# Two-step logits, a reordered stage-out, a split first chunk and a last block in pieces, in a TensorE-bound attention + MLP kernel

## The chip, the cores and the metric

One core of a Trainium2 chip. The metric is the device time of one execution in microseconds (us), as the median of several runs. The profile's span is about 1.7 us shorter than the time of the same run; I compare times with times and spans with spans.

## The reference, cut to what matters

```python
xn = layernorm(x)                              # x: 1 x 2048 x 1024
out = x + A(xn) + B(xn)
# A: 32 heads of 32, four segments of 512 tokens; per segment and head
#    p = softmax(q k^T * scale + causal mask); a_dot = p v
#    a_mem = phi(q) M / (phi(q) z);  M, z summed over earlier segments
#    o = g * a_mem + (1 - g) * a_dot;  A = o @ wo
# B: token-mixing MLP: u = gelu(layernorm(xn)^T w1 + b1); B = (u w2 + b2)^T
```

## The kernel before

TensorE (PE) computes the hidden layer first. Then come 32 units, each of four heads in one segment. Between the short pieces of a unit's attention the kernel places the long matmuls of w2 and wo ("main" matmuls), so that PE has work while ScalarE does exps. `share(u)` says how many main matmuls go into each gap. Main block c (128 tokens) sums half 0 in bank 6 and half 1 in bank 7; VectorE then drains each into a staging tile.

The logits of a unit use row tiles: head r occupies rows 32r to 32r+31 of the array, so four matmuls of 32 rows run at once (in the timeline below, four start within 0.01 us of each other). Key block kb has 128 keys and 512 - 128 kb queries. Before the change a unit has three such steps, all in banks 0 to 3, one bank a head. In the code, cut and shortened, `weigh` is the product of p and v:

```python
LOGIT_STEPS = [[0], [1], [2, 3]]
def logits(self, u, step):
    ...
    with fw.group(reads=[kT[k], qT[k]], writes=self.R_bank[0:4]):
        for kb in kbs:
            for r in range(4):
                fw.mm(self.ps[:, r, col:col + n_q], kT[32r:32r+32, kb*P:(kb+1)*P],
                      qT[32r:32r+32, kb*P:SEG_L], ..., tile_position=(32 * r, 0))
    # one exp of ScalarE per step, then one causal select of POOL per key block
# ... one unit:
self.logits(u, 0);  self.main_emit(n0)
self.logits(u, 1);  self.main_emit(n1)
self.logits(u, 2);  self.main_emit(n2)
self.weigh(u, 0); self.weigh(u, 1)     # banks 4 and 5
self.proj_q(un, 0)                     # bank 0
self.weigh(u, 2); self.proj_v(..., 2); self.weigh(u, 3)
self.proj_k(un, 1)                     # bank 1; VectorE copies k, then ScalarE takes exp(k)
self.main_emit(n3)                     # then the next unit's logits
```

The end of the kernel is eight products of o and wo in blocks of 128 tokens by 512 columns; VectorE adds each to what was staged out, and a DMA writes it. The start loads x in chunks; VectorE computes the statistics and writes h, and ten matmuls on zeros (the warm-ups) run on PE meanwhile.

The softmax here doesn't subtract the row's maximum and nothing guards it: scores larger than these inputs give would overflow.

Of the kernel before, what the change touches and what calls it, by code (L numbers as in the profile page):

```python
# [6 lines left out]
ACT = mybir.ActivationFunctionType  # L7
ALU = mybir.AluOpType
# [8 lines left out]
SEG_L = 512  # L17
# [12 lines left out]
N_UNIT = N_SEG * N_GRP  # L30
VW = D_HEAD + 1
GW = 4 * VW
PT_OFF = [0, 512, 896, 1152]
PT_COLS = 1280


# [66 lines left out]

class FW:
    N_DMA_SEMS = 64
    N_OUT_SEMS = 24
    N_OWN_SEMS = 16

    def __init__(self, nc, ctx):
# [236 lines left out]
class _Kernel:  # L346
# [31 lines left out]
    def alloc(self):  # L378
# [49 lines left out]
        self.w1early = nc.alloc_sbuf_tensor_at("w1early", [P, N_TCH, 512], BF16, offset=w1_at)  # L428
        self.late_end = e.at
        self.R_xin = [Res(f"xin{c}") for c in range(N_TCH)]  # L430
        self.R_xin0 = Res("xin0a")
        self.R_junk, self.R_warm = Res("junk"), Res("warm")
        self.R_h = [[Res(f"h{c}_{h}") for h in range(2)] for c in range(N_TCH)]
        self.R_hh = [[self.R_h[c][h] for c in range(N_TCH)] for h in range(2)]
# [79 lines left out]
    def consts(self):  # L514
        fw = self.fw
        fw.op("dve", lambda e: e.memset(self.warm[:], 0.0), writes=[self.R_warm])
        for brow, R in ((self.brow1, self.R_brow1), (self.brow2, self.R_brow2)):
            fw.op("dve", lambda e: e.memset(brow[:], 0.0), writes=[R[4]])
        self.w1_ring = _Ring(fw, [t[:] for t in self.w1ring], self.R_w1s, depth=2)
        for fp in range(N_FCH // 2):  # L520
            self.w1_ring.srcs.append(self.B_w1[:, fp * 256:(fp + 1) * 256].rearrange("(c p) f -> p c f", p=P))
        self.R_w1e = [Res(f"w1e{c}") for c in range(N_TCH)]
        for h in range(2):
            fw.dma(self.xin[:, 0, h * 512:(h + 1) * 512], self.x_d[:, 0, h * 512:(h + 1) * 512],
                   writes=[(self.R_xin0, self.R_xin[0])[h]], issuer=("sp", "act")[h])
        fw.op("act", lambda e: e.activation(self.junk[:, 0:1], self.warm[:, 0:1], ACT.Gelu_apprx_tanh),
              reads=[self.R_warm], writes=[self.R_junk])
        for kind, c0, n in (("x", 1, 1), ("x", 2, 1), ("x", 3, 1), ("w", 0, 2), ("x", 4, 2), ("w", 2, 2), ("x", 6, 2),
                            ("w", 4, 4), ("x", 8, 4), ("w", 8, 4), ("x", 12, 4), ("w", 12, 4)):
            if kind == "x":  # L530
                self.load_x(c0, n)
            else:
                self.fw.dma(self.w1early[:, c0:c0 + n, :],
                            self.B_w1[c0 * P:(c0 + n) * P, 0:512].rearrange("(c p) f -> p c f", p=P),
                            writes=self.R_w1e[c0:c0 + n], issuer="act" if c0 == 0 else "sp")
        self.w1_ring.issued = 2
        for brow, src, n, R in ((self.brow1, self.B_b1, N_FCH, self.R_brow1), (self.brow2, self.B_b2, N_TCH, self.R_brow2)):
            for j in range(4):
                fw.dma(brow[32 * j:32 * j + n, :], src.rearrange("(c q) -> c q", q=P)[:, 32 * j:32 * j + 32],
                       reads=[R[4]], writes=[R[j]])  # L540
        fw.dma(self.beta_sb[:], self.A_beta.partition_broadcast(P), writes=[self.R_beta])

        fw.op("pool", lambda e: e.memset(self.expo[:], -0.5), writes=[self.R_expo])
        fw.op("pool", lambda e: e.memset(self.ident[:], 0.0), writes=[self.R_ident])
        fw.op("pool", lambda e: e.affine_select(self.ident[:], self.ident[:], pattern=[[-1, P]],
                                                compare_op=ALU.not_equal, fill=1.0, base=0,
                                                channel_multiplier=1),
              reads=[self.R_ident], writes=[self.R_ident])
        with fw.group(reads=[self.R_warm], writes=[self.R_bank[0]]):
            for _ in range(self.N_WARM):  # L550
                fw.mm(self.bank(0), self.warm[:, 0:P], self.warm[:], start=True, stop=True)
# [65 lines left out]
    def stats_dve(self, c, halves):  # L617
        fw = self.fw
        src, st, R = self.xin[:, c, :], self.ln_st[:, c, :], self.R_st[c]
        for h in halves:  # L620
            R_x = self.R_xin0 if c == 0 and h == 0 else self.R_xin[c]
            fw.op("dve", lambda e: e.bn_stats(st[:, 6 * h:6 * h + 6], src[:, 512 * h:512 * h + 512]), reads=[R_x],
                  writes=[R])
        if halves[-1]:
            fw.op("dve", lambda e: e.bn_aggr(self.ln_mv[:, c, :], st.rearrange("p (a s) -> p a s", s=6)),
                  reads=[R], writes=[R])
# [29 lines left out]

    def scale_h(self, c):
        reads = [self.R_xin[c], self.R_st[c], self.R_rs[c]]
        for h0, h1 in ((0, 1), (1, 2)) if c == 1 else ((0, 2),):
            cols = slice(512 * h0, 512 * h1)  # L660
            self.fw.op("dve", lambda e: e.tensor_scalar(self.h[:, c, cols], self.xin[:, c, cols], self.ln_mv[:, c, 0:1],  # L661
                                                        self.ln_rs[:, c, 1:2], op0=ALU.subtract, op1=ALU.mult),
                       reads=reads, writes=self.R_h[c][h0:h1])
# [111 lines left out]
        self.fw.dma(self.pk[j][:], self.mtmp[1][:], reads=[self.R_mtmp[1]], writes=[self.R_pk[j]], transpose=True)  # L775


    LOGIT_STEPS = [[0], [1], [2, 3]]

    def logits(self, u, step):  # L780
        fw = self.fw
        k = u % 3
        kbs = self.LOGIT_STEPS[step]
        total = sum(SEG_L - P * kb for kb in kbs)
        with fw.group(reads=[self.R_kT[k], self.R_qT[k]], writes=self.R_bank[0:4]):
            col = 0
            for kb in kbs:
                n_q = SEG_L - P * kb
                for r in range(4):
                    fw.mm(self.ps[:, r, col:col + n_q], self.kT[k][32 * r:32 * r + 32, kb * P:(kb + 1) * P],  # L790
                          self.qT[k][32 * r:32 * r + 32, kb * P:SEG_L],
                          start=True, stop=True, tile_position=(32 * r, 0))
                col += n_q
        off = PT_OFF[kbs[0]]
        fw.op("act", lambda e: e.activation(self.pT[:, :, off:off + total], self.ps[:, 0:4, 0:total],  # L795
                                            ACT.Exp, scale=SCALE),
              reads=self.R_bank[0:4],
              writes=[self.R_pTu[kb] for kb in kbs] + [self.R_pTd[kb] for kb in kbs])
        for kb in kbs:
            d = self.pT[:, :, PT_OFF[kb]:PT_OFF[kb] + P]  # L800
            fw.op("pool", lambda e: e.affine_select(d, d, pattern=[[0, 4], [1, P]], compare_op=ALU.is_ge,  # L801
# [95 lines left out]
    def main_init(self):  # L897


        self.main = []  # L900
        for j, c in enumerate(self.mlp_order):
            self.main += [(j, c, half, a, a + 14) for half in range(2) for a in (0, 14)]
            if c < 12:
                self.main += [(j, c, half, N_FCH, N_FCH + N_GRP) for half in range(2)]
        self.main_k = 0
        self.main_at = 0

# [38 lines left out]
    def attention_and_out(self):  # L946
# [17 lines left out]
        for u in range(N_UNIT):  # L964
            s = u // N_GRP
            un, m = u + self.LEAD, u // 4 + 1
            n0, n1, n2, n3 = self.share(u)
            if u == N_GRP:
                wait = _after(*[self.R_xnT[c] for c in range(4)])
                self.oT[1] = self.xnT[0]  # L970
# [5 lines left out]
            if u and not last_of_seg(u - 1):  # L976
                self.combine(u - 1)
            self.logits(u, 1)
            self.main_emit(n1)
            self.logits(u, 2)  # L980
            if u + 1 < N_UNIT and (u + 1) // N_GRP < N_SEG - 1:
                self.k_transpose(u + 1)
            if u and not last_of_seg(u - 1):
                self.o_transpose_dma(u - 1)
            self.main_emit(n2)
            self.weigh(u, 0)
            self.weigh(u, 1)
            if un < N_UNIT:
# [8 lines left out]
                self.proj_k(un, 1)  # L997
            if last_of_seg(u):
                self.combine(u)
            self.main_emit(n3)  # L1000
        assert self.main_k == len(self.main)
        self.tail()

    @staticmethod
    def share(u):

        if u < N_UNIT - 4:
            return (10, 8, 7, 7) if u < N_GRP else (10, 8, 8, 8)
        return (10, 9, 8, 10) if u < N_UNIT - 2 else (10, 9, 8, 4)

    def tail(self):
        fw = self.fw
# [6 lines left out]
            fw.dma(fin[i][:], self.out_d[:, 4 * s + i, :], reads=[self.R_out[4 * s + i]], writes=R_fin[i],  # L1019
                   record_reads=False)  # L1020

        def product(n, j0, j1):
            i, h, b = n // 2, n % 2, (0, 1, 2, 3, 4, 5, 7, 6)[n]
            with fw.group(reads=[self.R_wo] + self.R_oT[s % 2][j0:j1], writes=[self.R_bank[b]]):
                for jc in range(j0, j1):
                    fw.mm(self.bank(b), self.oT[s % 2][:, jc, i * P:(i + 1) * P],
                          self.wo_sb[:, jc, h * 512:(h + 1) * 512], start=(jc == 0), stop=(jc == N_GRP - 1))
            if j1 < N_GRP:
                return
            dst = fin[i][:, h * 512:(h + 1) * 512]  # L1030
            fw.op("dve", lambda e: e.tensor_tensor(dst, self.bank(b), dst, op=ALU.add),  # L1031
                  reads=[self.R_bank[b], R_fin[i][h]], writes=[R_fin[i][h]])
            fw.dma(self.out_d[:, 4 * s + i, h * 512:(h + 1) * 512], dst, reads=[R_fin[i][h]],
                   writes=[self.R_out[4 * s + i]], is_output=True)

        product(0, 0, 7)
        product(1, 0, 7)
# [1 line left out]
        product(2, 0, 7)  # L1039
        for n in range(3):  # L1040
            product(n, 7, 8)
        for n in range(3, 8):
            product(n, 0, 8)


# [26 lines left out]
```

## Time and profile before

| | before |
|---|---|
| time, median of the first 3 runs | 704.21 us (703.87 to 705.7) |
| span of the profile | 702.2 us |
| PE busy | 688.9 us (98%) |
| first real matmul | 7.14 us |
| last PE work to end of span | about 3 us |

PE is the only engine near its limit. From the page (part 1, and the chain of work that ended last; PE is TensorE's matmuls, PEld its weight loads, DVE VectorE, ACT ScalarE, POOL GpSimd, SPq and ACTq the queues that issue DMAs, x the number of instructions):

```profile
PE 688.9 (98%) x4724; PEld 322.7 (46%) x4814; DVE 258.5 (37%) x578; ACT 277.5 (40%) x301; POOL 100.8 (14%) x156
...
PE 95%; DMA 1%; issue 1%; DVE 1%; SPq 0%; ACT 0%; ACTq 0%
```

"Busy" hides short gaps and waits, because matmul records overlap: a dense full matmul of 512 columns is recorded with 0.38 us, but the next one starts 0.216 us later. Start times do not hide them. Here are the three logits steps of a unit in segment 2, by the timeline (start, us busy, engine, line, operation, tiles, count, and the idle time before with what ended it):

```profile
486.04 0.10 PEld L194 LDWEIGHTS ps_all<-qT_1549,kT_1552 32*128 32x128 bf16 x4 [0.42 <-issue]
486.04 0.40 PE L194 MATMUL ps_all<-qT_1549,kT_1552 32*128 32x512 bf16 x4
486.37 1.90 PE L194 MATMUL ps_all<-gT,w2h_896 128*128 128x512 bf16 x8
...
488.64 0.34 PE L194 MATMUL ps_all<-qT_1549,kT_1552 32*128 32x384 bf16 x4
488.91 1.90 PE L194 MATMUL ps_all<-gT,w2h_895 128*128 128x512 bf16 x8
...
490.74 0.34 PE L194 MATMUL ps_all<-qT_1549,kT_1552 32*128 32x256 bf16 x8
```

The four tiled matmuls of a step start within 0.01 us of each other. The last full matmul before the step started 0.312 us earlier (single records; 0.216 when dense). The tiles' 512 columns need 0.213 us (a step with 128 columns fewer is 0.053 us shorter), yet the next full matmul starts 0.33 us after their start. So each step costs about 0.21 us beside its columns, 0.096 us on entry (0.312 less 0.216) and about 0.115 us on exit; the texts call an entry with its exit a switch.

One wait of PE on another engine stands out. It is in the chain between 377 and 381 us (start, us, what):

```profile
377.27 0.70 DVE kT_1552 L755
...
378.06 0.61 ACT etmp_1566 L758
...
378.69 0.30 DVE mtmp_1568 L726
...
379.62 0.75 DVE stg_1573 L939
...
380.51 0.59 PE ps_all L194 x2
...
PE ps_all L194 <- DVE stg_1573 L939: 0.7, 1, 0.7
```

Half 0's drain (`stg`) sits in VectorE's queue behind the copy of k and work that waits for ScalarE's exp. PE needs bank 6 for the next block and waits (0.85 us by start times; the last line is from the waits view: us in total, times, longest).

The end, by the timeline: the last add starts at 699.27 us; its transfer is issued and lands, and the span ends at 702.2.

```profile
696.70 2.54 PE L194 MATMUL ps_all<-wo_sb,xnT_70 128*128 128x512 bf16 x11
...
699.27 0.69 DVE L1031 TENSOR_TENSOR fin_7784<-ps_all,fin_7784 128x512 bf16<-128x512 f32 x1 [1.03 <-PE ps_all L194]
```

### The profile page before, as it was taken

The page shows a single profiled execution, that of the slowest core. Times are in us where ns is not written, and L with a number is a line of the kernel's source. Part 1 is how long each engine was busy: PE and PEld are TensorE (multiplying, and loading weights), DVE is VectorE, ACT ScalarE, POOL GpSimd, SP SyncE. Part 2 cuts the span into 40 slices and gives each one's busy share as a digit, 9 for nine tenths or more (in the row PEclk, how much of TensorE's full clock was granted, in tenths as well). Part 3 has the DMA queues.
Part 4 walks back from the last instruction along what each step waited for, and adds up shares of the span by engine and source line. Part 5 has one row for each costly group of instructions (what it writes and reads, how often), then busy time and mean ns, then how long its engine had stood idle before and what let it go on. Part 6 is the DMA issues. An engine that isn't in the chain of part 4 may idle for free.

```text
span 702.2 us, 11155 instructions
## 1 busy us (share of the span) xinstructions
PE 688.9 (98%) x4724; PEld 322.7 (46%) x4814; DVE 258.5 (37%) x578; ACT 277.5 (40%) x301; POOL 100.8 (14%) x156
## 2 busy tenths in 40 slices
PE   8999999999999999999999999999999999999998
PEld 3444444444444444444444444444444444444443
DVE  7730000000012333343454454545546553434444
ACT  7522111111134445444544444444444444443440
POOL 3600000000001111211121211112211111211120
DMA  9497694226044537556264543526173444537003
GB/s 323 98 225 176 139 234 125 61 60 139 1 159 92 114 60 145 120 94 118 50 133 98 112 100 75 128 46 143 34 170 88 86 95 78 114 69 120 23 16 135
DMA packets 210393, 77.17 MB, mean 110 GB/s; under 512 B 172840, under 2 KB 202792, under 8 KB 210344
## 3 DMA queue, kind: packets, MB, share of 16 engines
q1 hardware_dynamic: 209928, 76.06, 47.8%
q8 instruction: 38, 0.62, 0.4%
q10 hardware_dynamic: 416, 0.39, 0.2%
q14 instruction: 11, 0.09, 0.0%
HBM read 59.79 MB, written 5.24 MB: 93 GB/s over the span
## 4 chain that ended last, share of the span: by engine, by line
PE 95%; DMA 1%; issue 1%; DVE 1%; SPq 0%; ACT 0%; ACTq 0%
PE ps_all L194 95%; DMA xin<-in_A_x_dram 1%; SPq L216 0%; DVE prod L873 0%; DVE stg_1573 L939 0%; DVE stg_1571 L939 0%; DVE kT_1552 L755 0%; DVE fin_7784 L1031 0%; DVE ost_1562 L835 0%; ACT etmp_1566 L758 0%; DVE h L661 0%; DVE o_s_1564 L877 0%; PE ps_all L200 0%; DVE srec L871 0%; DVE mtmp_1568 L726 0%
## 5 line engine op out<-in xcount | busy, mean ns | idle before, releaser
L795 ACT ACTIVATE pT<-ps_all 128x1536 bf16<-128x1536 f32 (+1 forms) x96 | 152.9, 1593 | 93.9 <-PE ps_all L194 93.9
L801 POOL TENSOR_SCALAR_AFFINE_SELECT pT<-pT 128x512 bf16<-128x512 bf16 x128 | 84.6, 673 | 564.6 <-ACT pT L795 564.6
L717 ACT ACTIVATE gT<-ps_all,b1c 128x512 bf16<-128x512 f32 x56 | 37.7, 690 | 139.1 <-PE ps_all L194 133.6
L755 DVE CAST kT_1552<-ps_all 128x512 bf16<-128x512 f32 x11 | 7.6, 691 | 170.4 <-PE ps_all L194 170.4
L194 PE MATMUL ps_all<-h,w1s_80 128*128 128x512 bf16 x251 | 55.6, 379 | 0.3
L194 PE MATMUL ps_all<-h,w1s_81 128*128 128x512 bf16 x251 | 55.6, 379 | 0.3
L194 PE MATMUL ps_all<-h,w1s_79 128*128 128x512 bf16 x250 | 55.4, 379 | 0.3
L194 PE MATMUL ps_all<-gT,w2h_895 128*128 128x512 bf16 x219 | 55.1, 380 | 0.4 <-issue 0.2
L194 PE MATMUL ps_all<-gT,w2h_893 128*128 128x512 bf16 x220 | 53.9, 380 | 1.0 <-DVE stg_1573 L939 0.7
L194 PE MATMUL ps_all<-gT,w2h_894 128*128 128x512 bf16 x215 | 53.8, 380 | 0.9 <-issue 0.6
L194 PE MATMUL ps_all<-gT,w2h_896 128*128 128x512 bf16 x217 | 53.9, 380 | 0.6 <-issue 0.3
L835 DVE CAST ost_1561<-ps_all 128x264 bf16<-128x264 f32 (+1 forms) x64 | 23.8, 394 | 64.4 <-PE ps_all L194 64.2
L194 PEld LDWEIGHTS ps_all<-h,w1s_80 128*128 128x128 bf16 x256 | 25.0, 98 | 30.2
L194 PEld LDWEIGHTS ps_all<-h,w1s_79 128*128 128x128 bf16 x256 | 25.0, 98 | 30.2
L194 PEld LDWEIGHTS ps_all<-h,w1s_81 128*128 128x128 bf16 x256 | 25.0, 98 | 30.2
L758 ACT ACTIVATE etmp_1566<-ps_all 128x512 bf16<-128x512 f32 x24 | 14.3, 597 | 58.8 <-DVE kT_1554 L755 20.7
L835 DVE CAST ost_1562<-ps_all 128x264 bf16<-128x264 f32 (+1 forms) x64 | 23.7, 394 | 37.2 <-PE ps_all L194 37.0
L194 PEld LDWEIGHTS ps_all<-gT,w2h_893 128*128 128x128 bf16 x224 | 20.4, 98 | 26.6 <-issue 4.6
L194 PEld LDWEIGHTS ps_all<-gT,w2h_896 128*128 128x128 bf16 x224 | 20.4, 98 | 25.3 <-issue 3.5
L194 PEld LDWEIGHTS ps_all<-gT,w2h_894 128*128 128x128 bf16 x224 | 20.1, 98 | 25.2 <-issue 4.0
L194 PEld LDWEIGHTS ps_all<-gT,w2h_895 128*128 128x128 bf16 x224 | 20.0, 98 | 25.2 <-issue 4.5
L194 PE MATMUL ps_all<-wo_sb,oT_1569 128*128 128x512 bf16 x124 | 30.4, 380 | 0.3 <-issue 0.2
(154 smaller groups left out, 838.6 us busy)
## 6 DMA issues: line engine op xcount, KB each, us to landing
w1s_81<-in_B_w_dram SPq DMA_DIRECT2D x4, 1024.0 KB, 5.7
w1s_79<-in_B_w_dram SPq DMA_DIRECT2D x4, 1024.0 KB, 5.8
w1s_80<-in_B_w_dram SPq DMA_DIRECT2D x4, 1024.0 KB, 5.7
wq_889<-in_A_wq_dram SPq DMA_DIRECT2D x16, 256.0 KB, 4.5
wq_890<-in_A_wq_dram SPq DMA_DIRECT2D x16, 256.0 KB, 3.5
wk_891<-in_A_wk_dram SPq DMA_DIRECT2D x16, 256.0 KB, 4.8
wk_892<-in_A_wk_dram SPq DMA_DIRECT2D x16, 256.0 KB, 3.8
w2h_893<-in_B_w_dram SPq DMA_DIRECT2D x8, 448.0 KB, 4.8
```

The costliest lines, as they stand in the source:

```text
L194: ins = self.nc.tensor.matmul(*args, **kwargs)
L717: fw.op("act", lambda e: e.activation(self.gT[:, fc, half * 512:(half + 1) * 512], self.bank(b), ACT.Gelu_apprx_tanh, bias=self.b1c[:, fc: ...
L755: fw.op("dve", lambda e: e.tensor_copy(self.kT[k][:], self.bank(b)), reads=[self.R_bank[b]], writes=[self.R_kT[k]])
L758: fw.op("act", lambda e: e.activation(self.etmp[1][:], self.bank(b), ACT.Exp), reads=[self.R_bank[b]], writes=[self.R_etmp[1]])
L795: fw.op("act", lambda e: e.activation(self.pT[:, :, off:off + total], self.ps[:, 0:4, 0:total], ACT.Exp, scale=SCALE), reads=self.R_bank[0:4],
L801: fw.op("pool", lambda e: e.affine_select(d, d, pattern=[[0, 4], [1, P]], compare_op=ALU.is_ge, fill=0.0, base=0, channel_multiplier=-1), ...
L835: fw.op("dve", lambda e: e.tensor_copy(dst, self.ps[:, b, 0:n * VW]), reads=[self.R_bank[b]], writes=[self.R_ost[o][qb]])
```

## The change

It has four parts. (1) Two logits steps instead of three: key blocks 0 and 2, then 1 and 3. Key block 2's results go to banks 4 and 5, two heads in each. (2) Half 0's wo sum goes between the two parts of half 1's w2 sum, so bank 6 is drained earlier. (3) The first x chunk is split by partitions instead of columns over two queues, w1's first part moves to the other queue, and h of chunk 0 is written in halves. (4) The last 512 columns are computed, added and written in pieces of 256, 128 and 128.

```diff
-    LOGIT_STEPS = [[0], [1], [2, 3]]
+    LOGIT_STEPS = [[[(0, 2), (2, 2)], [(1, 0), (3, 0), (0, 0), (2, 0)], [(1, 2), (3, 2)]],
+                   [[(0, 1), (1, 1), (2, 1), (3, 1), (0, 3), (1, 3), (2, 3), (3, 3)]]]   # (head, key block)
...
+            if len(toks) == 2:        # the second pair waits for the first: same banks, other row tiles
+                fw.E["pe"].eng.wait_ge(toks[0].sem, toks[0].val)
...
-            return (10, 8, 7, 7) if u < N_GRP else (10, 8, 8, 8)
+            return (11, 14, 7) if u < N_GRP else (11, 15, 8)
...
-                self.main += [(j, c, half, N_FCH, N_FCH + N_GRP) for half in range(2)]
+                wo = [(j, c, half, N_FCH, N_FCH + N_GRP) for half in range(2)]
+                runs = runs[:3] + [wo[0], runs[3], wo[1]] if c % 4 else runs + wo
...
-            fw.dma(self.xin[:, 0, h * 512:(h + 1) * 512], ...)
+            fw.dma(self.xin[64 * h:64 * h + 64, 0, :], ...)
...
-        for h0, h1 in ((0, 1), (1, 2)) if c == 1 else ((0, 2),):
+        for h0, h1 in ((0, 1), (1, 2)) if c < 2 else ((0, 2),):
...
-        for n in range(3, 8):
+        for n in range(3, 7):
             product(n, 0, 8)
+        product(7, 0, 8, ((0, 256), (256, 384), (384, 512)))
```

More of the change, by code (lines that the diff above doesn't have):

```diff
@@ L32 @@
 GW = 4 * VW
-PT_OFF = [0, 512, 896, 1152]
+PT_OFF = [0, 768, 512, 1152]
 PT_COLS = 1280
@@ L105 @@
     N_DMA_SEMS = 64
-    N_OUT_SEMS = 24
+    N_OUT_SEMS = 26
     N_OWN_SEMS = 16
@@ L430, in alloc @@
         self.R_xin = [Res(f"xin{c}") for c in range(N_TCH)]
-        self.R_xin0 = Res("xin0a")
+        self.R_xin0 = Res("xin0b")
         self.R_junk, self.R_warm = Res("junk"), Res("warm")
@@ L522, in consts @@
         self.R_w1e = [Res(f"w1e{c}") for c in range(N_TCH)]
-        for h in range(2):
-            fw.dma(self.xin[:, 0, h * 512:(h + 1) * 512], self.x_d[:, 0, h * 512:(h + 1) * 512],
-                   writes=[(self.R_xin0, self.R_xin[0])[h]], issuer=("sp", "act")[h])
+        for h, issuer in enumerate(("sp", "act")):
+            fw.dma(self.xin[64 * h:64 * h + 64, 0, :], self.x_d[64 * h:64 * h + 64, 0, :],
+                   writes=[(self.R_xin[0], self.R_xin0)[h]], issuer=issuer)
         fw.op("act", lambda e: e.activation(self.junk[:, 0:1], self.warm[:, 0:1], ACT.Gelu_apprx_tanh),
               reads=[self.R_warm], writes=[self.R_junk])
-        for kind, c0, n in (("x", 1, 1), ("x", 2, 1), ("x", 3, 1), ("w", 0, 2), ("x", 4, 2), ("w", 2, 2), ("x", 6, 2),
+        for kind, c0, n in (("x", 1, 1), ("x", 2, 1), ("w", 0, 2), ("x", 3, 1), ("x", 4, 2), ("w", 2, 2), ("x", 6, 2),
                             ("w", 4, 4), ("x", 8, 4), ("w", 8, 4), ("x", 12, 4), ("w", 12, 4)):
@@ L534, in consts @@
                             self.B_w1[c0 * P:(c0 + n) * P, 0:512].rearrange("(c p) f -> p c f", p=P),
-                            writes=self.R_w1e[c0:c0 + n], issuer="act" if c0 == 0 else "sp")
+                            writes=self.R_w1e[c0:c0 + n])
         self.w1_ring.issued = 2
@@ L620, in stats_dve @@
         for h in halves:
-            R_x = self.R_xin0 if c == 0 and h == 0 else self.R_xin[c]
-            fw.op("dve", lambda e: e.bn_stats(st[:, 6 * h:6 * h + 6], src[:, 512 * h:512 * h + 512]), reads=[R_x],
+            reads = [self.R_xin[c]] + ([self.R_xin0] if c == 0 else [])
+            fw.op("dve", lambda e: e.bn_stats(st[:, 6 * h:6 * h + 6], src[:, 512 * h:512 * h + 512]), reads=reads,
                   writes=[R])
@@ L782, in logits, with weights @@
         k = u % 3
-        kbs = self.LOGIT_STEPS[step]
-        total = sum(SEG_L - P * kb for kb in kbs)
-        with fw.group(reads=[self.R_kT[k], self.R_qT[k]], writes=self.R_bank[0:4]):
-            col = 0
-            for kb in kbs:
-                n_q = SEG_L - P * kb
-                for r in range(4):
-                    fw.mm(self.ps[:, r, col:col + n_q], self.kT[k][32 * r:32 * r + 32, kb * P:(kb + 1) * P],
+        toks = []
+        for group in self.LOGIT_STEPS[step]:
+            if len(toks) == 2:
+                fw.E["pe"].eng.wait_ge(toks[0].sem, toks[0].val)
+            banks = self.R_bank[4:6] if group[0][1] == 2 else self.R_bank[0:4]
+            with fw.group(reads=[self.R_kT[k], self.R_qT[k]], writes=banks) as grp:
+                for r, kb in group:
+                    n_q = SEG_L - P * kb
+                    b, col = (4 + r // 2, 256 * (r % 2)) if kb == 2 else (r, 384 if kb == 3 else 0)
+                    fw.mm(self.ps[:, b, col:col + n_q], self.kT[k][32 * r:32 * r + 32, kb * P:(kb + 1) * P],
                           self.qT[k][32 * r:32 * r + 32, kb * P:SEG_L],
                           start=True, stop=True, tile_position=(32 * r, 0))
-                col += n_q
-        off = PT_OFF[kbs[0]]
-        fw.op("act", lambda e: e.activation(self.pT[:, :, off:off + total], self.ps[:, 0:4, 0:total],
-                                            ACT.Exp, scale=SCALE),
-              reads=self.R_bank[0:4],
-              writes=[self.R_pTu[kb] for kb in kbs] + [self.R_pTd[kb] for kb in kbs])
+            toks.append(grp.tok)
+        heads = self.ps[:, 0:4, :]
+        if step == 0:
+            self.weights((0,), heads, self.R_bank[0:4])
+            self.weights((2,), self.ps[:, 4:6, :].rearrange("p b (h q) -> p (b h) q", q=256), self.R_bank[4:6])
+        else:
+            self.weights((1, 3), heads, self.R_bank[0:4])
+    def weights(self, kbs, src, R_src):
+        fw = self.fw
+        off, total = PT_OFF[kbs[0]], sum(SEG_L - P * kb for kb in kbs)
+        fw.op("act", lambda e: e.activation(self.pT[:, :, off:off + total], src, ACT.Exp, scale=SCALE),
+              reads=R_src, writes=[self.R_pTu[kb] for kb in kbs] + [self.R_pTd[kb] for kb in kbs])
         for kb in kbs:
@@ L901, in main_init @@
         for j, c in enumerate(self.mlp_order):
-            self.main += [(j, c, half, a, a + 14) for half in range(2) for a in (0, 14)]
+            runs = [(j, c, half, a, a + 14) for half in range(2) for a in (0, 14)]
             if c < 12:
-                self.main += [(j, c, half, N_FCH, N_FCH + N_GRP) for half in range(2)]
+                wo = [(j, c, half, N_FCH, N_FCH + N_GRP) for half in range(2)]
+                runs = runs[:3] + [wo[0], runs[3], wo[1]] if c % 4 else runs + wo
+            self.main += runs
         self.main_k = 0
@@ L966, in attention_and_out @@
             un, m = u + self.LEAD, u // 4 + 1
-            n0, n1, n2, n3 = self.share(u)
+            n0, n1, n2 = self.share(u)
             if u == N_GRP:
@@ L978, in attention_and_out @@
             self.logits(u, 1)
-            self.main_emit(n1)
-            self.logits(u, 2)
             if u + 1 < N_UNIT and (u + 1) // N_GRP < N_SEG - 1:
@@ L984, in attention_and_out @@
                 self.o_transpose_dma(u - 1)
-            self.main_emit(n2)
+            self.main_emit(n1)
             self.weigh(u, 0)
@@ L999, in attention_and_out @@
                 self.combine(u)
-            self.main_emit(n3)
+            self.main_emit(n2)
         assert self.main_k == len(self.main)
@@ L1007, in share @@
         if u < N_UNIT - 4:
-            return (10, 8, 7, 7) if u < N_GRP else (10, 8, 8, 8)
-        return (10, 9, 8, 10) if u < N_UNIT - 2 else (10, 9, 8, 4)
+            return (11, 14, 7) if u < N_GRP else (11, 15, 8)
+        return (11, 16, 10) if u < N_UNIT - 2 else (11, 16, 4) if u < N_UNIT - 1 else (11, 13, 7)
     def tail(self):
@@ L1020, in tail, with product @@
                    record_reads=False)
-        def product(n, j0, j1):
+        def product(n, j0, j1, cols=((0, 512),)):
             i, h, b = n // 2, n % 2, (0, 1, 2, 3, 4, 5, 7, 6)[n]
-            with fw.group(reads=[self.R_wo] + self.R_oT[s % 2][j0:j1], writes=[self.R_bank[b]]):
-                for jc in range(j0, j1):
-                    fw.mm(self.bank(b), self.oT[s % 2][:, jc, i * P:(i + 1) * P],
-                          self.wo_sb[:, jc, h * 512:(h + 1) * 512], start=(jc == 0), stop=(jc == N_GRP - 1))
-            if j1 < N_GRP:
-                return
-            dst = fin[i][:, h * 512:(h + 1) * 512]
-            fw.op("dve", lambda e: e.tensor_tensor(dst, self.bank(b), dst, op=ALU.add),
-                  reads=[self.R_bank[b], R_fin[i][h]], writes=[R_fin[i][h]])
-            fw.dma(self.out_d[:, 4 * s + i, h * 512:(h + 1) * 512], dst, reads=[R_fin[i][h]],
-                   writes=[self.R_out[4 * s + i]], is_output=True)
+            for p, (c0, c1) in enumerate(cols):
+                with fw.group(reads=[self.R_wo] + self.R_oT[s % 2][j0:j1], writes=[self.R_bank[b]]):
+                    for jc in range(j0, j1):
+                        fw.mm(self.ps[:, b, c0:c1], self.oT[s % 2][:, jc, i * P:(i + 1) * P],
+                              self.wo_sb[:, jc, h * 512 + c0:h * 512 + c1], start=(jc == 0), stop=(jc == N_GRP - 1))
+                if j1 < N_GRP:
+                    return
+                dst = fin[i][:, h * 512 + c0:h * 512 + c1]
+                R = Res("fin")
+                R.w = R_fin[i][h].w
+                fw.op("dve", lambda e: e.tensor_tensor(dst, self.ps[:, b, c0:c1], dst, op=ALU.add),
+                      reads=[self.R_bank[b], R], writes=[R])
+                fw.dma(self.out_d[:, 4 * s + i, h * 512 + c0:h * 512 + c1], dst, reads=[R],
+                       is_output=True, issuer=("sp", "act")[p % 2])
+                b = (b + 1) % 3
         product(0, 0, 7)
```

## The prediction

> **What bounds the kernel now.** TensorE. The page gives PE 688.9 us busy of a 702.2 us span (98%), ACT 40%, DVE 37%; the chain of work that ended last is 95% PE. By start times in the timeline, full matmuls follow each other every 0.216 us from 7.14 us on. Beside that there is little: 7.1 us ahead of the first real matmul; entries to and exits from the row-tiled logits; one PE wait of 0.7 us for a stage-out add of VectorE (waits view, at 380 us); 0.4 us before the last transposes; 2.9 us after PE's last matmul.
>
> **The logits.** A unit has three row-tiled steps. The last full matmul before a step starts 0.312 us before the first tiled one (0.216 in dense streaming); the next full matmul comes 0.105 us later than the tiles' streaming accounts for, its successor 0.01 late: 0.21 us a step, 96 steps, 20 us. [...] The change has two steps: 32 x 0.21 = 6.7 us removed. The streamed columns stay 1280 per tile.
>
> But the new first step holds a wait: key block 2's four heads share banks 4 and 5, and the second pair waits for the first's completion[...]. A tiled 256-column matmul takes 0.277 us to its end, plus 0.04 us to the waiter (as PE to ACT shows), so the second pair starts 0.32 us into the step instead of 0.215. I estimate 0.10 to 0.15 us returned per unit, 3.2 to 4.8 us. Net gain: 2 to 3.5 us.
>
> Exps: 1.88 + 1.45 + 1.45 us become 1.88 + about 1.0 + 1.88, the same sum; by my estimate ScalarE frees the banks 0.5 us before step two needs them, and POOL's selects (0.63 us each) are done 0.5 us before the weighing. No effect.
>
> **Stage-out order.** With the first half's wo sum amid the second half's w2, bank 6 is drained long before it is needed: the 0.7 us wait (0.85 in the start gap) goes.
>
> **Start.** The first chunk was already on two queues; a split by partitions should land alike (3.64 and 3.82 us before). Statistics now need both halves (up to 0.15 us later); the first half of h takes 0.36 instead of 0.53 us. w1's first part, now behind x chunk 2, should land near 5.9 us, in time. First matmul 0.0 to 0.3 us earlier, 0.1 expected; PE is dense after it.
>
> **Tail.** The last add shrinks from 0.69 us (512 columns) to about 0.22 (128), the last transfer from 128 to 32 KB saves perhaps 0.1, narrow matmuls cost 0.06: 0.5 us. The 0.4 us before the transposes stays.
>
> **Sum.** 704.2 - 2.7 - 0.8 - 0.1 - 0.5 = about 700.1 us; 697.2 to 703.2 should hold it. Within 2%: 0.97; faster by over 2%: 0.02; slower: 0.01.
>
> **Checks.** Right: two switches a unit; each first step's last pair about 0.32 us after the first; unit period 0.06 to 0.11 us shorter; no PE wait at 380 us; PE end to span end 2.4 us. Wrong: the inner wait costs over 0.2 us (no gain) or nothing (gain near 6 us); PE waiting for ACT or POOL at step two or the weighing; a later first matmul.
>
> **What would break it.** A slower restart after the inner wait; POOL selects of 0.9 us, seen sometimes, delaying the weighing; the earlier stage-out add delaying the key copy and thereby the next logits.

The sum: 2.7 + 0.8 + 0.1 + 0.5 = 4.1 us off 704.2, about 700.1. The 0.21 us was read from the trace; that the second pair has to wait was the premise, and no run tested it. The wait's 0.277 and 0.04 us can be read in the trace of before: a tiled matmul of 256 columns is recorded with 0.277 to 0.278 us, and ScalarE starts 0.04 to 0.05 us after the PE work it waits for. The terms of the tail were estimates, without their source: 0.22 us for the last add, 0.1 for the transfer, 0.06 for the narrow matmuls. The traces of before and after show 0.29 us for the add, 0.24 less from its end to the end of the span (2.24 to 2.00), and 0.04 more for the matmuls (eight times 0.109 + 2 x 0.056 us from start to start, against eight times 0.216).

## The result, and the profile after

The changed kernel took 699.52 us (median of 4 runs, 698.74 to 700.99) against 704.77 (703.87 to 705.7). The ratio is 0.9928, interval 0.9904 to 0.9951. A ratio here is the mean time of one kernel's runs over that of the other's of the same rounds, so it is not quite the ratio of the medians. The gain is 0.7%, within the 2% to which the prediction gave 0.97. The two profiled spans are 702.2 and 698.3 us.

PE's busy time, from the page, hardly moved:

```profile
PE 687.9 (99%) x4740; PEld 327.3 (47%) x4830; DVE 260.3 (37%) x581; ACT 273.9 (39%) x301; POOL 104.8 (15%) x156
```

The gain is in gaps. The waits view of PE no longer has the stage-out add (line: who waited for whom, us in total, times, longest):

```profile
PE ps_all L194 <- DVE h L661: 1.5, 1, 1.5
PE ps_all L194 <- DVE brow_51 L518: 1.3, 1, 1.3
PE ps_all L200 <- DVE o_s_1566 L890: 0.5, 1, 0.5
PE ps_all L194 <- issue: 0.3, 2, 0.2
```

The two steps of a unit in segment 2, by the timeline:

```profile
574.61 0.11 PEld L194 LDWEIGHTS ps_all<-qT_1551,kT_1554 32*128 32x128 bf16 x6 [0.42 <-DVE srec L885]
574.61 0.63 PE L194 MATMUL ps_all<-qT_1551,kT_1554 32*128 32x256 bf16 x8
574.95 0.09 PEld L194 LDWEIGHTS ps_all<-qT_1551,kT_1554 32*128 32x128 bf16 x2 [0.24 <-PE ps_all L194]
575.15 2.79 ACT L810 ACTIVATE pT<-ps_all 128x2048 bf16<-128x2048 f32 x2 [3.98 <-PE ps_all L194]
575.17 0.98 PEld L194 LDWEIGHTS ps_all<-gT,w2h_895 128*128 128x128 bf16 x6
...
577.65 0.40 PE L194 MATMUL ps_all<-qT_1551,kT_1554 32*128 32x384 bf16 x8
...
577.98 0.82 PE L194 MATMUL ps_all<-gT,w2h_896 128*128 128x512 bf16 x3
```

Step one shows the wait inside: six weight loads run at once, two come 0.34 us later, released by PE itself. That is the second pair, waiting for the first. The releaser in the first line (a small VectorE operation) is a guess of the profile; the 0.42 us there is the same at every entry.

From the single matmul records, per unit: three entries of 0.312 us and three steps of 0.327, 0.274 and 0.276 us (first tiled start to next full start) became two entries of 0.312 and two steps of 0.561 and 0.330. After a step the next full matmul takes 0.226 instead of 0.216 us. Together 3 x (0.312 - 0.216) + 0.877 + 0.030 = 1.195 us became 2 x 0.096 + 0.891 + 0.020 = 1.103: 0.092 us less a unit, 2.9 us in 32 units.

The unit period (start of a unit's logits to the next) confirms it in segments 1 and 2: 15.19 to 15.09 us. In segment 0 it fell by more, 14.65 to 14.43. The timeline of before shows why, in a unit of segment 0:

```profile
274.00 0.60 ACT L758 ACTIVATE etmp_1566<-ps_all 128x512 bf16<-128x512 f32 x1 [2.55 <-DVE kT_1554 L755]
...
274.71 0.13 PEld L194 LDWEIGHTS ps_all<-qT_1550,kT_1553 32*128 32x128 bf16 x4 [0.52 <-issue]
274.74 0.40 PE L194 MATMUL ps_all<-qT_1550,kT_1553 32*128 32x512 bf16 x4
```

Here the entry takes 0.432 us, not 0.312: the tiled loads wait until ScalarE has read bank 1 (274.00 + 0.60). In the changed kernel the first pair goes to banks 4 and 5, so it starts on time, and only the four matmuls behind it wait. The same place after:

```profile
274.67 0.60 ACT L758 ACTIVATE etmp_1568<-ps_all 128x512 bf16<-128x512 f32 x1 [2.55 <-DVE kT_1556 L755]
275.28 0.44 PEld L194 LDWEIGHTS ps_all<-qT_1552,kT_1555 32*128 32x128 bf16 x8 [0.42 <-issue]
275.29 0.63 PE L194 MATMUL ps_all<-qT_1552,kT_1555 32*128 32x256 bf16 x8
```

The entry is 0.311 us again, and the step is 0.561 us as in segment 2: the late bank hides behind the wait for the pair, which is there anyway. The late entry is in units 1 to 8 of the kernel before (unit 8 is the first of segment 1), 8 x 0.12 = 0.96 us. In unit 8 of the changed kernel 0.12 us come back: one start gap before a wo matmul (337.26 to 337.59 us) is 0.332 instead of 0.216 us, perhaps for a transpose of o that landed at 337.45; this was not tested. Net: 0.84 us.

The tail after:

```profile
693.63 2.36 PE L194 MATMUL ps_all<-wo_sb,xnT_70 128*128 128x512 bf16 x26
...
695.14 0.74 DVE L1047 TENSOR_TENSOR fin_7812<-ps_all,fin_7812 128x256 bf16<-128x256 f32 x2 [0.18 <-PE ps_all L194]
695.91 0.35 ACTq L216 DMA_DIRECT2D out_dram<-fin_7812  x1
696.03 0.29 DVE L1047 TENSOR_TENSOR fin_7812<-ps_all,fin_7812 128x128 bf16<-128x128 f32 x1 [0.16 <-PE ps_all L194]
```

The last add takes 0.29 instead of 0.69 us. From the last matmul's start to the end of the span 3.35 us became 2.54, but that start lies 0.20 us later after the transposes (three short pieces end later than seven full matmuls begin). Net: 0.6 us.

And the start went the wrong way. The first real matmul came at 7.20 us instead of 7.14, and the matmuls after it ran at half rate (about 0.43 us from start to start, against 0.216). The timeline of PE up to 10 us has 14 of them before and 7 after:

```profile
7.14 3.18 PE L194 MATMUL ps_all<-h,w1early 128*128 128x512 bf16 x14 [1.86 <-DVE h L661]
```

and after

```profile
7.20 3.01 PE L194 MATMUL ps_all<-h,w1early 128*128 128x512 bf16 x7 [1.49 <-DVE h L661]
```

```
start-to-start of the first real matmuls, us (from the trace's single records)
before: 7.14 | 0.215 0.215 0.215 0.215 0.215 0.216 ...
after:  7.20 | 0.38 0.43 0.43 0.43 0.43 0.43 0.33 0.22 ...
```

That cost 1.34 us in this run (36.16 us to the first matmul after the early hidden stage, where 7.20 us plus 128 matmuls at 0.216 would give 34.82).

So the work behind the start and the start itself must be read apart. The marker is the first matmul that uses the ring of w1 tiles, right after the early hidden stage. "Rest" is the span less this marker; the two profiles have 667.44 and 662.16 us, 5.28 less:

| profile | marker at | rest | rest against before |
|---|---|---|---|
| before | 34.76 | 667.44 | |
| after | 36.16 | 662.16 | -5.28 |
| logits_only | 36.40 | 663.40 | -4.04 |
| order_only | 34.71 | 666.59 | -0.85 |
| tail_only | 35.09 | 666.83 | -0.61 |
| start_only | 36.54 | 667.45 | 0.01 |
| eight_before_logits | 36.37 | 667.26 | -0.18 |
| no_second_pair | 34.74 | 658.61 | -8.83 |
| warm14 | 34.98 | 662.14 | -5.30 |
| warm4 | 36.93 | 662.15 | -5.29 |
| pair_in_step_two | 35.01 | 661.41 | -6.03 |
| start_by_columns | 34.68 | 662.13 | -5.31 |
| product_before_transposes | 35.98 | 661.68 | -5.76 |
| all_together | 34.98 | 660.97 | -6.47 |

Three profiles of the same code behind the start (after, warm14, warm4) agree within 0.03 us, so the rest can be read to some hundredths. The marker moves by over 2 us between runs.

### The profile page after: what moved, and what is told of

The parts are those of the page before. It is cut to its first block, busy times and chain, and to the rows that moved or that the text cites. A ratio compares the mean times of both kernels' runs of the same rounds, so it can differ in the third digit from the quotient of the medians.

```text
span 698.3 us, 11182 instructions
## 1 busy us (share of the span) xinstructions
PE 687.9 (99%) x4740; PEld 327.3 (47%) x4830; DVE 260.3 (37%) x581; ACT 273.9 (39%) x301; POOL 104.8 (15%) x156
## 4 chain that ended last, share of the span: by engine, by line
PE 96%; DMA 1%; issue 1%; DVE 1%; SPq 1%
PE ps_all L194 96%; DMA xin<-in_A_x_dram 1%; SPq L216 1%; DVE prod L886 0%; DVE stg_1573 L954 0%; DVE ost_1564 L848 0%; DVE h L661 0%; DVE o_s_1566 L890 0%; PE ps_all L200 0%; DVE srec L884 0%; DVE fin_7812 L1047 0%; DVE srec L883 0%; DVE srec L885 0%; DVE ln_mv L644 0%; DVE ln_st L622 0%
## 5 line engine op out<-in xcount | busy, mean ns | idle before, releaser
L810 ACT ACTIVATE pT<-ps_all 128x2048 bf16<-128x2048 f32 (+1 forms) x96 | 149.4, 1591 | 58.3 <-PE ps_all L194 57.2
L814 POOL TENSOR_SCALAR_AFFINE_SELECT pT<-pT 128x512 bf16<-128x512 bf16 x128 | 88.3, 703 | 554.8 <-ACT pT L810 553.7
L194 PE MATMUL ps_all<-gT,w2h_897 128*128 128x512 bf16 x219 | 54.3, 380 | 0.4
L194 PE MATMUL ps_all<-gT,w2h_895 128*128 128x512 bf16 x221 | 53.7, 380 | 0.2
L194 PE MATMUL ps_all<-gT,w2h_896 128*128 128x512 bf16 x214 | 53.0, 380 | 0.6 <-issue 0.2
L194 PE MATMUL ps_all<-gT,w2h_898 128*128 128x512 bf16 x215 | 52.7, 379 | 0.5 <-issue 0.2
L194 PEld LDWEIGHTS ps_all<-gT,w2h_898 128*128 128x128 bf16 x224 | 21.1, 98 | 25.5 <-issue 1.3
L194 PEld LDWEIGHTS ps_all<-gT,w2h_896 128*128 128x128 bf16 x224 | 20.9, 98 | 25.8 <-issue 1.7
L194 PEld LDWEIGHTS ps_all<-gT,w2h_895 128*128 128x128 bf16 x224 | 20.8, 98 | 25.2 <-issue 1.3
L194 PEld LDWEIGHTS ps_all<-gT,w2h_897 128*128 128x128 bf16 x224 | 20.7, 98 | 24.9 <-issue 1.3
```

The costliest lines, as they stand in the source:

```text
L194: ins = self.nc.tensor.matmul(*args, **kwargs)
L810: fw.op("act", lambda e: e.activation(self.pT[:, :, off:off + total], src, ACT.Exp, scale=SCALE), reads=R_src, writes=[self.R_pTu[kb] for ...
L814: fw.op("pool", lambda e: e.affine_select(d, d, pattern=[[0, 4], [1, P]], compare_op=ALU.is_ge, fill=0.0, base=0, channel_multiplier=-1), ...
```

## The experiments

Twelve kernels ran, in three groups. Each group shared runs of the kernel before, whose medians were 704.15, 704.12 and 705.71 us. The comparison with the reference does not vouch for small errors in the attention part.

### Each part alone, on the kernel before

The edits are the four parts of the diff above, one at a time.

> The kernel before with the two-step logits (and their shares of other matmuls) alone. My theory: per unit 0.09 us less in the switches (three entries and exits of 0.21 us become two, less 0.13 us of wait for the first pair inside step one), 2.9 us in 32 units; and in units 1 to 7 the 0.12 us wait for bank 1 (ScalarE's exp of the k projection) disappears behind the first pair, 0.8 us more: 3.5 to 4.0 us less than before in a like clock phase. If the bank wait is not part of it: 2.9 us. If the prediction's sum was right as it stood, 2 to 3.5 us. Unit period in segment 0: 14.64 to 14.43 us; in segment 1: 15.19 to 15.10 us.

Measured: 701.58 us (699.81 to 701.88), ratio 0.9946 (0.9927 to 0.9964). Unit period 14.43 us in segment 0 and 15.09 to 15.10 in segment 1, as expected. The rest is 4.04 us shorter: 2.9 for the switches, 0.84 net for the hidden bank wait (0.12 in each of eight units, less 0.12 that unit 8 gives back, here too), and 0.23 because the stage-out wait, still there, shrank from 0.85 to 0.62 us. Both terms of the theory are confirmed; the sum of the prediction for this part, 2 to 3.5, was too small.

> The kernel before with the first half's wo sum placed amid the second half's w2 sum, alone. My theory: only the PE wait at 380 us for the stage-out add disappears, 0.85 us less; every other gap between matmul starts stays as it is. Rival: the order does nothing by itself, and the wait went because the two-step logits shifted the units' work: then within 0.2 us of before, with the wait at 380 us still in the waits view.

Measured: 704.06 us (703.04 to 705.18), ratio 0.9989 (0.9973 to 1.0006). The rest is 0.85 us shorter, the unit period that held the wait went from 16.04 to 15.19, and the waits view has no stage-out add. The order does it by itself. On top of the two-step logits it is worth what they leave, 0.62 us.

> The kernel before with the last block in column pieces alone. From the last full matmul's start, 3.34 us to the end of the span before against 2.52 us with pieces: 0.7 to 0.8 us less, of it about 0.4 the add (0.69 to 0.29 us), 0.15 the shorter matmul, 0.2 the smaller transfer. If only the add counts: 0.4 us. If the narrower pieces of 256 and 128 columns slow PE by weight loads, the gain is under 0.3 us.

Measured: 703.53 us (703.22 to 706.85), ratio 0.9992 (0.9973 to 1.0012). From the last matmul's start to the end 2.54 us against 3.35, as expected; but the expectation forgot that this start lies 0.20 us later. The rest is 0.61 us shorter. In the trace the matmuls of 256 and 128 columns start every 0.109 and 0.056 us, so the weight loads do not slow them.

> The kernel before with the start changes alone (first chunk split by partitions, h of the first chunk in halves, w1's first part on the other queue). My theory: first real matmul at 7.1 to 7.3 us against 7.14 before, so nothing gained (within 0.2 us) when the clock is in a like phase[...]. Rival: the start changes cause the half rate that the changed kernel's trace showed up to 9.9 us; then all runs of this kernel are about 1.3 us slower than before and the trace shows 0.43 us spacing after 7.2 us.

Measured: 705.06 us (704.13 to 705.72), ratio 1.0002 (0.9986 to 1.0018). Three runs lie at 704.1 to 704.5 and three at 705.6 to 705.7, and only the profiled run, one of the upper three, is seen to run at half rate (until 10.43 us). By the times, then, the half rate comes and goes within one kernel: the start changes do not cause it as such. They gain nothing. The first real matmul came at 7.46 us, outside the 7.1 to 7.3 expected. In the profiles, the later half of the first chunk landed at 3.40 to 3.82 us when split by columns (7 traces) and at 3.87 to 4.21 us, with one at 3.78, when split by partitions (7 traces). The first real matmul came at 7.05 to 7.47 us (median 7.09) with the columns and at 7.12 to 7.46 (median 7.38) with the partitions, so the split rather costs time; the kernels differ in other things too, and the ranges overlap.

The parts add up: 4.04 + 0.62 (order behind logits) + 0.61 (tail) + 0 (start) = 5.27 us; the measured difference of the rest is 5.28.

### What the wait inside step one costs

```diff
-    LOGIT_STEPS = [[[(0, 2), (2, 2)], [(1, 0), (3, 0), (0, 0), (2, 0)], [(1, 2), (3, 2)]],
+    LOGIT_STEPS = [[[(0, 2), (2, 2)], [(1, 0), (3, 0), (0, 0), (2, 0)]],
...
-            self.weights((2,), self.ps[:, 4:6, :].rearrange("p b (h q) -> p (b h) q", q=256), self.R_bank[4:6])
+            self.weights((2,), self.ps[:, 4:6, None, 0:256].to_broadcast([P, 2, 2, 256]), self.R_bank[4:6])
```

> The changed kernel without the second pair of key block 2 (heads 1 and 3) and so without the wait for the first pair; ScalarE reads the first pair's banks twice, so its work is the same. Wrong result on purpose. My theory: the pair's columns would run free beside the other row tiles, and the wait alone makes step one 0.56 us long from its first tiled matmul to the next full one; without it 0.43 to 0.44 us: 0.125 us a unit, 4.0 us in all less than the changed kernel. Rival: the step is long because of the columns or of the bank change, not of the wait: then 0.50 us or more, under 2 us in all.

Measured: 696.19 us (695.18 to 697.09). The timeline of the two steps' PE lines:

```profile
570.32 0.50 PE L194 MATMUL ps_all<-qT,kT 32*128 32x256 bf16 x6
570.75 2.55 PE L194 MATMUL ps_all<-gT,w2h 128*128 128x512 bf16 x11
```

Step one is 0.43 us long instead of 0.56, and 0.45 in segment 0, where the late bank 1 now shows. Over the 31 unit periods this is 3.8 us; the rest is 3.55 us shorter than the changed kernel's, because the stretch from the last unit to the transposes came out 0.27 us longer. There PE, being early, waits for a DMA transpose of o, while the gap of 0.41 us before the last transposes is gone. From its waits view:

```profile
PE ps_all L194 <- DMA xnT<-o_s: 0.7, 1, 0.7
```

The edit removes the pair's 256 columns together with the wait, so by itself it does not show that the columns would have been free. The other steps do: a step is as long as the columns of its longest tile ask, 0.274 us for 384, 0.327 for 512 and 0.43 for 768, and 0.433 also where 256 of the 768 are in two tiles alone (step two of pair_in_step_two, below). With the pair, step one has 768 columns in every tile. So the wait costs 0.13 us, of the 0.21 us that a removed step saves. In the trace of after, the second pair starts 0.347 us into the step. From the 0.213 us for 512 columns I estimate that without the wait it could start at about 0.22, after key block 0 in tiles 1 and 3. No run kept the pair and left out the wait, so whether the result needs the wait was not shown.

### The bank wait in segment 0

```diff
-            return (10, 8, 7, 7) if u < N_GRP else (10, 8, 8, 8)
+            return (10, 8, 6, 8) if u < N_GRP else (10, 8, 8, 8)
```

> The kernel before with one matmul moved in each unit of segment 0, from before the weighing to just before the next unit's logits (shares 10, 8, 6, 8 for 10, 8, 7, 7). My theory: the entry into the first logits step of units 1 to 7 takes 0.43 us because bank 1 is still being read by ScalarE (exp of the k projection); 0.22 us later it is free and the entry takes 0.312, so the unit period in segment 0 falls from 14.65 to 14.53 us, 0.8 to 1.0 us in all. Rival: the 0.43 us is a record missing from the trace or part of the mode switch: then nothing changes.

Measured: 705.21 us (703.73 to 708.06), ratio 1.0009 (0.9988 to 1.0029). The entry fell from 0.432 to 0.311 us, so the wait for bank 1 was real and not a missing record. But the unit period fell only from 14.65 to 14.63, and the rest by 0.18 us. The timelines show where the gain went, at the projection of q behind the weighing. In the kernel before:

```profile
279.84 1.45 ACT L795 ACTIVATE pT<-ps_all 128x1536 bf16<-128x1536 f32 x1 [0.66 <-PE ps_all L194]
...
281.52 0.98 PEld L194 LDWEIGHTS ps_all<-xnT_70,wq_889 128*128 128x128 bf16 x6
```

and in eight_before_logits:

```profile
281.37 1.45 ACT L795 ACTIVATE pT<-ps_all 128x1536 bf16<-128x1536 f32 x1 [0.66 <-PE ps_all L194]
...
282.94 0.34 PEld L194 LDWEIGHTS ps_all<-xnT,wq 128*128 128x128 bf16 x3
```

With one matmul less ahead of it, the projection reaches bank 0 before the exp of step three has read it (281.37 + 1.45 = 282.82; before, 281.29, and the projection comes 0.23 us later). It starts 0.127 us after the last weighing matmul; in the kernel before it was 0.025. One wait was traded for another. The gain of the expectation failed; its reason held. The changed kernel does better here because its first pair needs no late bank.

### The levels: the granted clock

The 37 runs of the kernel before lie at 703.83 to 704.24 us (19 of them), 704.88 to 706.30 (14) and 707.01 to 707.72 (4). The trace of logits_only explains the first two. Its windows view (stretch; busy us and count of each engine; granted clock; DMA share; GB/s):

```profile
core 0: us, PE busy (x) PEld busy (x) DVE busy (x) ACT busy (x) POOL busy (x), PEclk, DMA share, GB/s
0.00:3.90 3.90, 2.64 (x7) 0.99 (x8) 0.73 (x4) 1.49 (x2) 0.74 (x7) 1.00 0.49 149
3.90:7.40 3.50, 1.32 (x7) 0.46 (x6) 2.75 (x8) 2.60 (x5) 0.58 (x2) 1.00 1.02 353
7.40:10.80 3.40, 3.40 (x10) 1.21 (x8) 3.19 (x10) 3.28 (x6) 1.62 (x3) 0.50 1.06 376
10.80:14.20 3.40, 3.40 (x18) 1.50 (x16) 3.14 (x10) 3.24 (x6) 1.10 (x3) 1.00 1.05 376
```

PEclk is 0.50 in one stretch of 3.4 us that holds 10 matmuls instead of 16. (In the first row it reads 1.00 although the warm-ups started every 0.427 us: the record begins with the first change of the clock.) The changes are at 3.96, 7.37 and 10.78 us, 3.41 apart; in eight_before_logits at 4.17, 7.58 and 10.99. The changes keep no fixed time from the start ("free-running" in the expectation below): the warm-ups begin at 1.25 to 1.26 us in all traces, but the first change of the clock lies anywhere from 3.96 to 6.87 us where it comes before the real work (3.96 in logits_only, 4.17 in eight_before_logits, 4.98 in warm14), and at 9.94 us in after. A stretch of 3.41 us at half rate should cost half of that, 1.7 us by this arithmetic; in logits_only it cost 1.67 us (marker at 36.40 us, where 7.08 us plus 128 matmuls at 0.216 would give 34.73).

The traces also show what PE did before a change. In logits_only and eight_before_logits it had a gap of 2.18 and 2.06 us ahead of the real work, and half rate began at 7.37 and 7.58 us. In before the gap was 1.86 us, and the matmuls after it start every 0.215 to 0.216 us. An estimate from the start times and modelled ends: in the 3.41 us before the change to full rate at 3.96 us (logits_only) PE was busy for 79%, in those before the change to half rate for 36% (logits_only) and 40% (eight_before_logits). In after, counted back from 9.94 us, it was busy for 76% of the 3.41 us that end at 6.52 us, and the rate stayed at half. A share of busy time that decides it was not shown.

```diff
-    N_WARM = 10
+    N_WARM = 14        # warm14;  4 in warm4
```

> The changed kernel with 14 warm-up matmuls instead of 10. My theory: the runs of every kernel fall into levels about 1.7 us apart because the array runs its first real matmuls at half rate until the end of a free-running window of about 3.4 us[...]; 10 warm-ups (4.3 us cold) miss it in some runs, 14 (6.0 us) never do. So all runs within 0.5 us of 698.8, none near 700.5, and the trace has 0.216 us spacing from the first real matmul at 7.2 us. Rival: the levels have another cause (DMA, launch): then two levels as before.

Measured: 698.86 us, all six runs between 698.60 and 699.08; ratio 0.9918 (0.9904 to 0.9932). In the trace the clock went to full rate at 4.98 us and the real matmuls start every 0.216 us from 7.36. The upper level is gone, as the theory says, and it did not show in the 20 runs of the four kernels below, which have 14 warm-ups too. Ten warm-ups at half rate keep PE busy for about 4.4 us (1.26 to 5.71 us in after). In after they ended before the clock had changed; in logits_only it had changed at 3.96 us, and with PE idle from 4.90 to 7.08 us it fell back at 7.37. Fourteen keep PE busy until 6.2 to 7.2 us (five traces); that this is why the upper level is gone is the reading, which the times of warm14 and warm4 bear out. The same stretch of the timeline as above, up to 10 us:

```profile
7.36 2.96 PE L194 MATMUL ps_all<-h,w1early 128*128 128x512 bf16 x13 [1.09 <-DVE h L661]
```

> The changed kernel with 4 warm-up matmuls instead of 10. My theory: [...]every run starts its real matmuls at half rate, for 2.5 to 6 us: every run is 1.3 to 3.0 us above the low level of 698.8, at 700.1 to 701.8, with 0.427 us spacing after 7.2 us in the trace. Rival (levels have another cause): the same levels as with 10.

Measured: 700.92 us, all four runs between 700.82 and 701.40. Half rate until 11.29 us in the trace, 3.88 us from the first real matmul at 7.41. Every run is at the high level, as the theory says and its rival does not.

Without the chance of the clock, the change is worth 5.2 us: the low runs are 703.87 and 704.21 before, 698.74 and 698.99 after, in the same rounds. The level of the four runs at 707 to 707.7 us is open: no profile fell on it.

### Towards a better version, all with 14 warm-ups

These four kernels ran on another chip than warm14, in another round. The lowest run of the kernel before is 703.83 us in warm14's group and 703.89 in this one; still, the rests of the traces are the firmer comparison. The edits, cut:

```diff
+    # pair_in_step_two
-    LOGIT_STEPS = [[[(0, 2), (2, 2)], [(1, 0), (3, 0), (0, 0), (2, 0)], [(1, 2), (3, 2)]],
-                   [[(0, 1), (1, 1), ... (3, 3)]]]
+    LOGIT_STEPS = [[[(0, 2), (2, 2)], [(1, 0), (3, 0), (0, 0), (2, 0)]],
+                   [[(1, 2), (3, 2)], [(0, 1), (1, 1), ... (3, 3)]]]     # exp of key block 2 moved there as well; one main matmul moved in the last unit
+    # start_by_columns: chunk 0 and w1's first part loaded as in the kernel before; h of chunk 0 in halves
+    # product_before_transposes
-        self.o_transpose(u, 6)
         product(2, 0, 7)
-        for n in range(3):
+        self.o_transpose(u, 6)
+        product(3, 0, 7)
+        for n in range(4):
             product(n, 7, 8)
-        for n in range(3, 7):
+        for n in range(4, 7):
             product(n, 0, 8)
```

> The changed kernel with 14 warm-ups, and the second pair of key block 2 moved from the end of step one to the head of step two (its exp after the other one there). The first pair is then long done, so nothing waits inside a step, but row tiles 1 and 3 stream 256 columns more in step two. My theory: step one 0.43 us (0.45 in segment 0, where bank 1 is late), step two 0.43, together 0.87 us against 0.56 + 0.33 = 0.89: 0.02 us a unit, 0.5 to 0.8 us less than warm14's 698.86 in all. Rival: the moved exp delays the weighing's bank 4 and gives more back: no gain or slower.

Measured: 698.18 us (697.88 to 698.36). Steps of 0.429 (0.449 in segment 0) and 0.433 us; unit period 15.07 against 15.09; rest 0.73 us shorter than warm14's. Step two streams 256 columns more in two of the tiles, and the two steps together are still 0.03 us shorter than with the wait (0.862 against 0.891).

> The changed kernel with 14 warm-ups and the start of the kernel before (first chunk by columns, w1's first part on ScalarE's queue), h of the first chunk still in halves. My theory: statistics start on the first half alone, about 0.3 us sooner than with the split by partitions, so the first real matmul comes 0.1 to 0.35 us earlier than warm14's, but not before the warm-ups end; 0.1 to 0.3 us less than warm14 in all. Rival: the landing times scatter more than that: no difference beyond 0.1 us.

Measured: 698.62 us (698.45 to 699.25). First real matmul at 7.05 us in its trace against 7.36. By the median 0.24 us less than warm14, but the ranges overlap, so this is not settled. In its trace and in that of all_together (7.36 us) the statistics of chunk 0 end early, but the write of h waits in VectorE's queue behind the statistics of chunk 2, whose data landed at 5.88 and 6.18 us. Moving h ahead of those statistics was not tried.

> The changed kernel with 14 warm-ups and the seven matmuls of the third closing product put ahead of the last transposes instead of behind them (the fourth's seven behind). My theory: PE has 1.5 us more of work while VectorE finishes the last combine, so the 0.41 us gap before the transposes goes and nothing else changes: 0.4 us less than warm14. Rival: the transposes' copy or the product's banks then make PE wait as long elsewhere: no gain.

Measured: 698.54 us (698.23 to 699.39). The timelines at the last transposes, warm14 first:

```profile
680.14 2.97 PE L194 MATMUL ps_all<-wo_sb,xnT 128*128 128x512 bf16 x13
683.58 0.40 PE L200 MATMUL ps_all<-ident,o_s 128*128 128x128 bf16 x4 [0.46 <-DVE o_s L890]
```

and product_before_transposes:

```profile
681.11 4.69 PE L194 MATMUL ps_all<-wo_sb,xnT 128*128 128x512 bf16 x21
685.64 0.39 PE L200 MATMUL ps_all<-ident,o_s 128*128 128x128 bf16 x4
```

The gap is gone and the rest is 0.46 us shorter. Its profiled run is the slowest of the five: PE waited once (0.97 us from one early matmul to the next, at full rate) for the h of chunk 2. VectorE wrote that only at 11.13 us, behind the statistics of chunk 4, whose data landed at 10.50 us (8.3 to 10.1 in the other traces). That is the data, not the clock.

> The changed kernel with 14 warm-ups, the second pair in step two, the start by columns and the product before the transposes. My theory: the gains add, 1.0 to 1.5 us less than warm14's 698.86, so 697.3 to 697.9, and no run at a slow start level. Rival: one of them gives its gain back: 698 or more.

Measured: 697.71 us (697.38 to 698.06), ratio 0.9891 (0.9873 to 0.9910) against before. The rest is 1.17 us shorter than warm14's, about the sum of 0.73 and 0.46. Only three of the eleven runs of the kernel before in this group lie on its low level (703.89 to 704.13 us), so the ratio flatters: against these three the gain is 6.3 us, 0.9%. It is faster than both kernels of the study, and its runs scatter less.

## Why the prediction was right or wrong, point by point

The predicted 700.1 us and range of 697.2 to 703.2 hold the measured 699.52. Some of that is balance: the gain behind the start was larger than predicted, and the half rate at the start hid part of it.

- **The switches: right.** Predicted 2 to 3.5 us net; 2.9 measured. The wait inside was estimated at 0.10 to 0.15 us and is 0.13 (no_second_pair). The second pair starts at 0.347 us, not at 0.32.
- **"Unit period 0.06 to 0.11 us shorter": right in segments 1 and 2 (0.09), wrong in segment 0 (0.22).** The step that failed was to read the entry of 0.312 us in one unit of segment 2 and apply it to all 96 steps. In units 1 to 8 the first entry was 0.432 us, a wait for bank 1, and the new order hides it: 0.84 us net that the sum lacked.
- **Exps and selects: right.** The changed kernel's waits view shows no wait of PE or of its weight loads for ScalarE or POOL.
- **Stage-out: right in kind.** The wait went; alone it is worth 0.85 us, behind the new logits 0.62 (0.8 predicted).
- **Tail: right, 0.6 us for 0.5.** The last add took 0.29 us, not 0.22. The last PE end to span end is 2.3 us (2.4 predicted): the last matmul starts at 695.78 us and takes 0.22, and the span ends at 698.3.
- **Start: wrong.** "First matmul 0.0 to 0.3 us earlier, 0.1 expected; PE is dense after it" was 0.06 us later in the profile and 0.32 in that of start_only, whose times show no gain. The split by partitions did not land alike: the statistics of chunk 0 ended 0.30 us later in the profile (5.50 us against 5.20), and the half-size write of h (0.36 us for 0.53) won part of it back. And "dense" took the rate of the one trace at hand for granted: the time of the clock's changes, a term of up to 1.9 us here (warm4: marker at 36.93 us, where 7.41 us plus 128 matmuls at 0.216 would give 35.06), was not in the sum at all.

## What to carry to other kernels

PE was 98% busy here, and the gain was in the entries, exits and short waits between its instructions; measure them from start to start in every stage, not in one unit, before multiplying by the count. A wait that stays can hide another one behind it if the work that needs the late resource is put second (here 0.12 us in each of eight units); and moving work to remove one wait is worth little if the next one is 0.1 us away (0.18 us of the 0.8 to 1.0 expected in eight_before_logits). If the runs of a kernel fall into levels, look at the start: 14 warm-ups for 10, with TensorE idle for 1.09 us before the real work (warm14) instead of 1.49 to 2.18 (after, before, logits_only), made the runs agree within 0.5 us (warm14; 0.5 to 1.2 us in the four kernels after it, where late data remained).
